# Seven products instead of eight in the second layer of the last half of expert 3, normalising at another place, and a new table of moves

## The chip, the cores and the metric

The kernel runs on one core of a Trainium2 chip. The metric is the device time of one execution in microseconds (us), median of three runs. The core's engines run side by side, each through its own queue in order: PE (TensorE, matrix products), DVE (VectorE), ACT (ScalarE), POOL (GpSimd) and SP (SyncE, which issues most DMAs). They wait for each other through semaphores only.

## What is computed

Linear attention, a mixture of four experts ("first MoE"), and a two-layer network with an ELU ("second MoE"), one after the other:

```python
q_s = softmax(q over head_dim);  k_s = softmax(k over seq)          # 4 x 8 heads, 576 x 64
x = q_s @ (k_s.T @ v)                                               # -> 2304 tokens x 512
p = domain_probs / (domain_probs.sum(-1, keepdims=True) + 1e-09)    # 2304 x 4
for e in range(4):
    out += p[:, e:e + 1] * (relu(x @ w1[e]) @ w2[e])                # 512 -> 1024 -> 512
h = out @ w_in                                                      # 512 -> 2048
g = where(h > 0, h, exp(min(h, 0)) - 1)
result = g @ w_out                                                  # 2048 -> 512
```

## The kernel before

All matrix operands stand as pairs of a high and a low part, so each product of 128x128 weights with a block of tokens takes three matmuls (high x high, high x low, low x high). Sums are kept transposed (features on partitions) in one big tile, `accs`.

**The opening** does the attention (`START` and the hooks of `at(n, ...)`) beside expert 0, which runs over 7 blocks of 256 tokens and one of 512 without any saving of products. `matmul` counts columns and calls `hook()` after each 2048 of them; `at(n, fn)` puts `fn` at the n-th hook (a hook is about 1 us of PE). `normalise` divides the expert probabilities by their sum, in four small DVE instructions (L757 to L760); it stands at hook 10. `p_turn` (hook 150) transposes what it made and stores it to DRAM (`prow`).

**The main loop** has 30 steps, `STEPS`: `s` from 0 to 9, each with three token blocks `b` of 768 (step number i = 3 s + b). An `s` is half a unit, that is 4 slices of 128 hidden features: s = 0 to 5 are experts 1 to 3, s = 6 to 9 the second MoE. `S_MOE` is 6 and `S_FAST` is 5. In each step PE does the first layer of its own block by seven products (Strassen, `PRODUCTS`, done for each of two halves `fp` = 0, 1: 2 x 7 x 6 = 84 matmuls of 384 columns, line L1458), and between these the second layer of the step before, cut in pieces (`fill`):

- plain (`group`, L1546 to L1548): 8 groups of 12 matmuls, 96 in all. Before, s = 5 and the first block of s = 6 are done so.
- by seven products (`second_product`, L1670, or `turned_product`, L1583, in the second MoE): 7 x 12 = 84 matmuls. It needs sums and differences of quarters of the hidden values and of the second weights: `quarter_a11`, `direct`, `quarter_a21`, `quarter_a12`, `late_parts` for the values, and `w2_fast` for the weights. What comes out is weighted with `pb` and added to `accs` by DVE, or by DVE and POOL ("part").

The list `SEVEN` says which `s` are done by seven. Plain ones take their second weights whole, split in `w2_step`.

**Between the MoEs** the sums in `accs` become the next input. `own_steps(b)` does this for each block in seven pieces (B11, B21, T3, B22, T2, T4, T1): `hi` (L1226) makes the high part on ACT, `lo` (L1234) the low part on DVE or POOL, `diff` (L1242 to L1256) the differences in place on POOL, `keep` (L1262) stores each part to DRAM for the later steps. Block b's pieces stand in the second half of the step ahead of (s = 6, b) and in the first half of that step. A place in the ring of eight pieces is written again only when its store has read it.

The order on every engine is that in which the program is written out; the scheduler is off. Positions are counted in hooks (`at`), in `SH` = 24 places per step (`at2`, `hook2`) and in products (`drain`). The table `MOVES` shifts single operations by some places, or gives them another engine ('d' DVE, 'p' POOL, 'a' ACT).

A bank of PSUM that PE has filled is read by ACT and DVE before PE may write it again; so every sum, ReLU or ELU that is late holds PE a few products later. In the second MoE the ELU of one quarter is three ACT instructions (`elu`, L1500 to L1502) and two or more on DVE (`rest`, L1511 to L1518).

Of the kernel before, what the change touches and what calls it, by code (L numbers as in the profile page):

```python
# [62 lines left out]
    ('spe', 2, 14): 'd', ('spe', 2, 2): 'd', ('sprd', 0, 3): -0.5, ('sprd', 1, 10): 1, ('sprd', 1, 11): 1,  # L63
    ('sprd', 1, 12): 1, ('sprd', 1, 13): 1, ('sprd', 1, 14): 1, ('sprd', 1, 15): 1, ('sprd', 1, 16): 1,
    ('sprd', 1, 17): 1, ('sprd', 1, 4): 1, ('sprd', 1, 5): 1, ('sprd', 1, 6): 1, ('sprd', 1, 7): 1, ('sprd', 1, 8): 1,
    ('sprd', 1, 9): 1, ('sprd', 2, 10): 0.5, ('sprd', 2, 11): 0.5, ('sprd', 2, 12): 0.5, ('sprd', 2, 13): 0.5,
    ('sprd', 2, 14): 0.5, ('sprd', 2, 15): 0.5, ('sprd', 2, 16): 0.5, ('sprd', 2, 17): 0.5, ('sprd', 2, 5): 0.5,
    ('sprd', 2, 6): 0.5, ('sprd', 2, 7): 0.5, ('sprd', 2, 8): 0.5, ('sprd', 2, 9): 0.5, ('sumlo', 'T2'): 'p',
# [37 lines left out]
def tile_attention_moe_moe(  # L106
# [963 lines left out]
    def w2_step(s, p):  # L1070
# [6 lines left out]
        if s == S_MOE:  # L1077
            now = hook2_n[0] - NB * S_FAST * SH
            for n in range(2):
                at2(NB * S_FAST, now + 3 + n, lambda n=n: sums_of(r, p, n), "sm", p, n)  # L1080
# [808 lines left out]
```

## Time and profile before

| | |
|---|---|
| median of three runs | 1176.66 us (1175.61 to 1178.84) |
| the profiled execution, its own time | 1175.68 us |
| its span in the trace | 1173.7 us |
| busy share | PE 98%, DVE 81%, POOL 56%, ACT 54% |
| opening, until the first product of the loop | 261 us |
| one step of 84 + 84 matmuls without loss | 29.12 us |

A busy share of 98% is not 98% of work: matmuls overlap, and the end of each is modelled. What tells more is how many matmuls start in a stretch: at full pace those of 384 columns start every 173 ns. Steps that take longer than that have lost time.

### The profile page before, as it was taken

What the parts mean: (1) busy time and instruction counts of PE and PEld (TensorE: products, weight loads), DVE (VectorE), ACT (ScalarE), POOL (GpSimd) and SP (SyncE); (2) the same over time, 40 slices, a digit from 0 to 9 for tenths busy, and PEclk for the clock granted to TensorE, in tenths of its full rate; (3) what the DMA queues carried; (4) which work ended last, traced back from release to release, by engine and by line L of the source; (5) the groups of instructions that cost most, each with busy time, mean ns of one, the idle gap of its engine ahead of it and who ended that gap; (6) DMA issues with size and microseconds to landing.
All of it is one profiled execution on the core that took longest, in us unless ns stands there. A gap on an engine that the chain in (4) does not pass through costs nothing. (4 is left out here: it accounts for less than half of the span.)

```text
span 1173.7 us, 20319 instructions
## 1 busy us (share of the span) xinstructions
PE 1148.1 (98%) x7234; PEld 1127.7 (96%) x7234; DVE 949.9 (81%) x1514; ACT 638.5 (54%) x1348; POOL 659.1 (56%) x559
## 2 busy tenths in 40 slices
PE   8899999999999999999999999999989999999998
PEld 7899999989999999999999999999979999999998
DVE  8977888676887887898998987686478879879876
ACT  7544543325455455455455443245688767767763
POOL 5521543447578578577578572155755646646643
PEclk9999999999999999999999999999999999999999
DMA  9356565867677777767867869643575465565462
GB/s 287 121 151 197 164 216 189 297 232 267 243 252 268 273 244 277 275 233 281 293 238 269 301 222 326 240 186 115 187 247 194 180 251 206 196 235 207 180 242 108
DMA packets 124728, 266.76 MB, mean 227 GB/s; under 512 B 12428, under 2 KB 48980, under 8 KB 124628
## 3 DMA queue, kind: packets, MB, share of 16 engines
q1 hardware_dynamic: 122900, 262.33, 63.8%
q10 hardware_dynamic: 1728, 3.15, 0.7%
q8 instruction: 57, 0.93, 0.3%
q14 instruction: 43, 0.35, 0.1%
HBM read 218.21 MB, written 47.22 MB: 226 GB/s over the span
## 5 line engine op out<-in xcount | busy, mean ns | idle before, releaser
L1458 PE MATMUL m<-xh,w1s 128*128 128x384 f32 x840 | 246.5, 338 | 9.1 <-DVE half L1512 4.0
L1458 PE MATMUL h<-xh,w1s 128*128 128x384 f32 x840 | 243.7, 335 | 3.5 <-DVE half L1517 1.2
L1458 PEld LDWEIGHTS m<-xh,w1s 128*128 128x128 f32 x840 | 155.1, 189 | 13.4 <-DVE half L1512 4.3
L1458 PEld LDWEIGHTS h<-xh,w1s 128*128 128x128 f32 x840 | 154.3, 188 | 5.2 <-ACT m L1747 1.8
L1458 PE MATMUL m<-xl,w1s 128*128 128x384 f32 x420 | 141.3, 336 | 0.0
L1458 PE MATMUL h<-xl,w1s 128*128 128x384 f32 x420 | 140.6, 335 | 0.0
L1288 PE MATMUL o<-hpa,w2t 128*128 128x256 f32 (+1 forms) x768 | 119.8, 300 | 0.8 <-DVE hpa L1321 0.7
L1288 PE MATMUL h<-xh,w1t 128*128 128x256 f32 (+1 forms) x512 | 112.0, 298 | 0.0
L1288 PEld LDWEIGHTS o<-hpa,w2t 128*128 128x128 f32 x768 | 104.3, 191 | 5.5 <-DVE hpa L1321 1.0
L1696 POOL TENSOR_TENSOR accs<-part,accs 128x768 f32<-128x768 f32 x35 | 69.2, 1977 | 63.0 <-DVE part L1695 60.3
L1288 PEld LDWEIGHTS h<-xh,w1t 128*128 128x128 f32 x512 | 86.2, 192 | 2.5
L995 POOL TENSOR_TENSOR w2g<-r,w2g 128x512 fp32r<-128x512 f32 x54 | 73.8, 1378 | 14.9 <-ACT w2g L994 14.0
L1670 PE MATMUL o<-xh,w2g 128*128 128x384 f32 x360 | 79.8, 334 | 0.0
L1458 PEld LDWEIGHTS m<-xl,w1s 128*128 128x128 f32 x420 | 79.4, 189 | 0.2
L1458 PEld LDWEIGHTS h<-xl,w1s 128*128 128x128 f32 x420 | 78.8, 188 | 0.1
L1670 PE MATMUL o<-hpa,w2g 128*128 128x384 f32 x360 | 78.5, 335 | 0.0
L1670 PE MATMUL o<-xl,w2g 128*128 128x384 f32 x360 | 77.9, 335 | 0.0
L1288 PE MATMUL h<-xl,w1t 128*128 128x256 f32 (+1 forms) x256 | 77.5, 303 | 0.1
L1596 DVE TENSOR_TENSOR accs<-o,accs 128x768 f32<-128x768 f32 (+1 forms) x69 | 62.6, 908 | 4.7 <-PE o L1583 4.6
L1670 PEld LDWEIGHTS o<-hpa,w2g 128*128 128x128 f32 x360 | 63.8, 188 | 0.4 <-DVE o L1689 0.4
L1670 PEld LDWEIGHTS o<-xh,w2g 128*128 128x128 f32 x360 | 64.0, 188 | 0.0
L1670 PEld LDWEIGHTS o<-xl,w2g 128*128 128x128 f32 x360 | 63.7, 188 | 0.1
(364 smaller groups left out, 3002.8 us busy)
## 6 DMA issues: line engine op xcount, KB each, us to landing
xh<-xs SPq DMA_DIRECT2D x189, 384.0 KB, 6.4
xl<-xs SPq DMA_DIRECT2D x189, 384.0 KB, 6.8
xs<-xh SPq DMA_DIRECT2D x42, 384.0 KB, 3.5
xs<-xl SPq DMA_DIRECT2D x42, 384.0 KB, 3.8
r<-in_w_dram SPq DMA_DIRECT2D x56, 256.0 KB, 4.2
extra<-prow SPq DMA_DIRECT2D x38, 192.0 KB, 6.0
r<-scratch SPq DMA_DIRECT2D x24, 256.0 KB, 4.8
x<-in_w_in_dram SPq DMA_DIRECT2D x11, 512.0 KB, 6.0
```

The lines of the kernel that those rows point to most:

```text
L995: eng_of(nc.gpsimd, "w2lo", cls(s), op).tensor_tensor(out=t[:, 1], in0=src, in1=t[:, 0].bitcast(F32), op=ALU.subtract)
L1288: nc.tensor.matmul(out, lhsT, rhs, **kw)
L1458: nc.tensor.matmul(dst, t[:, wl, c + dl, :], x[xl_][:, dl, :], start=(n == 0 and p < 2), stop=(n == 5), skip_group_check=True,)
L1596: nc.vector.tensor_tensor(out=a, in0=x, in1=a, op=ALU.add)
L1670: nc.tensor.matmul(o[:, m], l, r, start=(k < 2 and n == 0), stop=(n == 5), skip_group_check=True)
L1696: nc.gpsimd.tensor_tensor(out=a, in0=r, in1=a, op=ALU.add)
```

## The change

Four edits:

- `SEVEN[s]` is now true for all s but 6. The second layer of s = 5 (steps 15 to 17) is done by `second_product`, its values by the quarters of the first MoE, its weights by `w2_fast`. The scratch tiles of step 17's last products are taken from `gt`, since the ELU of step 18 already uses the usual ones.
- The plain weights of s = 6 were loaded and split ahead of their step, during s = 5; now they are loaded and split in step 18 itself (`w_load(s, ., 1)`, `w2_step`, and behind it `sums_of`).
- `normalise` goes from hook 10 to hook 120. The last three conversions of second-MoE weights from 64-bit words use their usual tiles instead of `gt`.
- `MOVES` is laid out anew: 365 entries become 856, most with fractions of a place.

```diff
-    ('a11', 1, 1): 'd', ('ahead', 'E', 2, 0): 1, ('ahead', 'E', 2, 3): 1, ('ahead', 'E', 2, 8): 1,
+    ('a11', 1, 1): 'p', ('a11', 2, 1): 'd', ('ahead', 'M', 0, 1): 1, ('ahead', 'M', 0, 2): 1, ('ahead', 'M', 0, 6): 1,
...
-    SEVEN = [s < S_FAST or s > S_MOE for s in range((NU - 1) * FPU // FS)]
+    SEVEN = [s != S_MOE for s in range((NU - 1) * FPU // FS)]
...
-    at(10, normalise)
+    at(120, normalise, "nrm")
...
         if s == S_MOE:
-            now = hook2_n[0] - NB * S_FAST * SH
+            now = hook2_n[0] - NB * S_MOE * SH
             for n in range(2):
-                at2(NB * S_FAST, now + 3 + n, lambda n=n: sums_of(r, p, n), "sm", p, n)
+                at2(NB * S_MOE, now + 3 + n, lambda n=n: sums_of(r, p, n), "sm", p, n)
...
-    CONV += [(later, end1 + t, 1, True) for t in (11, 22, 33)]
+    CONV += [(later, end1 + t, 1, False) for t in (11, 22, 33)]
...
-            a2, b2, c2, d2, a1, b1 = (2, 13, 25, 29, 34, 38)
-            if s > 0 and (s <= S_FAST or SEVEN[s]):
+            a1, b1 = (34, 38)
+            if s > 0:
                 at2(i, 2, lambda s=s: w_load(s, 0, 1), "l", k_, 0)
                 at2(i, 13, lambda s=s: w_load(s, 1, 1), "l", k_, 1)
                 if SEVEN[s]:
...
                     at2(i, 14, lambda s=s: w2_step(s, 0), "ws", k_, 0)
                     at2(i, 19, lambda s=s: w2_step(s, 1), "ws", k_, 1)
-                    a2, b2, c2, d2, a1, b1 = (23, 26, 30, 34, 41, 54)
...
-            if more and not SEVEN[s] and not SEVEN[s + 1]:
-                at2(i, a2, lambda s=s: w_load(s + 1, 0, 1), "l", k_, 2)
-                at2(i, b2, lambda s=s: w_load(s + 1, 1, 1), "l", k_, 3)
-                at2(i, c2, lambda s=s: w2_step(s + 1, 0), "ws", k_, 2)
-                at2(i, d2, lambda s=s: w2_step(s + 1, 1), "ws", k_, 3)
...
-        if s == S_FAST:
-            summed.add((b, th, m))
...
-            sums["s5"] = tmp.tile([P, 2, TB], F32, tag="qh", name="m5")
+            sums["s5"] = gt[:, :2] if i == NB * S_MOE - 1 else tmp.tile([P, 2, TB], F32, tag="qh", name="m5")
...
-                r = tmp.tile([P, 2, TB], F32, tag="ql", name="part")
+                r = gt[:, 2:] if i == NB * S_MOE - 1 else tmp.tile([P, 2, TB], F32, tag="ql", name="part")
```

The changed file has some 120 lines more ahead of the code, so its line numbers are higher: L1234 (`lo` of `own_steps`) becomes L1352, L1242 to L1256 (`diff`) L1360 to L1374, L1511 and L1512 (`rest`) L1629 and L1630, L1751 and L1762 (the two sums of the first layer) L1869 and L1880.

**Place 1: DVE in the opening, at hook 10.** Before, with `normalise` in L757 to L760; `xl<-m,xh` and `hpa<-m,hpa` split what PE has turned or multiplied for the attention.

```order
L1321 SCALAR_TENSOR_TENSOR hpa<-h,hpa 128x256
L336 TENSOR_REDUCE nm<-accs 128x1
L484 TENSOR_TENSOR hpa<-m,hpa 128x288
L757 TENSOR_REDUCE gx_93<-gx_93 128x18
L758 TENSOR_SCALAR gx_93<-gx_93 128x18
L759 RECIPROCAL gx_93<-gx_93 128x18
L760 TENSOR_TENSOR gx_93<-gx_93 128x18x4
L506 TENSOR_TENSOR xl<-m,xh 128x288
L1321 SCALAR_TENSOR_TENSOR hpa<-h,hpa 128x256
L506 TENSOR_TENSOR xl<-m,xh 128x288
L438 TENSOR_REDUCE qm<-accs 96x12
```

The changed kernel at the same place, and behind it the new place of `normalise` at hook 120 (L881 to L884).

```order
L460 TENSOR_REDUCE nm<-accs 128x1
L608 TENSOR_TENSOR hpa<-m,hpa 128x288
L577 TENSOR_REDUCE accs<-accs 96x6
L578 TENSOR_SCALAR accs<-accs 96x6
L579 RECIPROCAL accs<-accs 96x6
L1439 SCALAR_TENSOR_TENSOR hpa<-h,hpa 128x256
L671 TENSOR_TENSOR w1t<-r,w1t 128x512
L608 TENSOR_TENSOR hpa<-m,hpa 128x288
L630 TENSOR_TENSOR xl<-m,xh 128x288
L562 TENSOR_REDUCE qm<-accs 96x12
L1439 SCALAR_TENSOR_TENSOR hpa<-h,hpa 128x256
L630 TENSOR_TENSOR xl<-m,xh 128x288
```

```order
L1439 SCALAR_TENSOR_TENSOR hpa<-h,hpa 128x256
L550 SCALAR_TENSOR_TENSOR kvs<-m,ks,kvs 64x64 x2
L1439 SCALAR_TENSOR_TENSOR hpa<-h,hpa 128x256
L881 TENSOR_REDUCE gx_93<-gx_93 128x18
L882 TENSOR_SCALAR gx_93<-gx_93 128x18
L883 RECIPROCAL gx_93<-gx_93 128x18
L884 TENSOR_TENSOR gx_93<-gx_93 128x18x4
L562 TENSOR_REDUCE qm<-accs 96x12
L483 TENSOR_TENSOR ek<-m,ek 128x640
L957 TENSOR_TENSOR xl<-sum,xh 128x2x384
```

The four instructions have left the place ahead of the splits (L506, now L630), a weight split (L671) stands nearer there, and they now stand among q's and k's late steps.

**Place 2: POOL from the second half of step 18 on.** Before: `own_steps` of block 1 (L1234, L1242 to L1256) between the splits of the ELU (L1482, `parts`).

```order
L1234 TENSOR_TENSOR xl<-accs,xh 128x768
L1482 TENSOR_TENSOR xh<-half,xh 128x384
L1242 TENSOR_TENSOR accs<-accs 128x768
L1234 TENSOR_TENSOR xl<-accs,xh 128x768
L1247 TENSOR_TENSOR accs<-accs 128x768
L1252 TENSOR_TENSOR accs<-accs 128x768
L1234 TENSOR_TENSOR xl<-accs,xh 128x768
L1482 TENSOR_TENSOR xl<-half,xl 128x384
L1234 TENSOR_TENSOR xl<-accs,xh 128x768
L1482 TENSOR_TENSOR xh<-half,xh 128x384
L1482 TENSOR_TENSOR hpa<-half,hpa 128x384
L1256 TENSOR_TENSOR accs<-accs 128x768
```

The changed kernel, the same stretch (L1199 `w2_step`, L1143 `sums_of`, L1814 the weighted part of step 17's second layer, L1600 `parts`, L1352 and L1370 `own_steps`).

```order
L1600 TENSOR_TENSOR hpa<-half,hpa 128x384
L1199 TENSOR_TENSOR w2s<-r,w2s 128x512 x2
L1143 TENSOR_TENSOR r<-r 128x256 x2
L1814 TENSOR_TENSOR accs<-gt,accs 128x768
L1370 TENSOR_TENSOR accs<-accs 128x768
L1600 TENSOR_TENSOR xl<-half,xl 128x384
L1600 TENSOR_TENSOR xh<-half,xh 128x384
L1352 TENSOR_TENSOR xl<-accs,xh 128x768
L1600 TENSOR_TENSOR xh<-half,xh 128x384
L1352 TENSOR_TENSOR xl<-accs,xh 128x768
L1600 TENSOR_TENSOR gx<-half,gx 128x384
L1352 TENSOR_TENSOR xl<-accs,xh 128x768
```

Of the eleven instructions of block 1 four are left on POOL (three `lo`, one `diff`); over the three blocks 19 become 9. The split of the weights of s = 6 and part of the new second layer have come in.

**Place 3: DVE in the second half of step 18.** Before (L1554 and L1555 weight and add the plain second layer of step 17).

```order
L1511 SCALAR_TENSOR_TENSOR m<-m,half 128x384
L1512 SCALAR_TENSOR_TENSOR half<-half,m 128x384
L1554 TENSOR_TENSOR o<-o,extra 128x384
L1555 TENSOR_TENSOR accs<-o,accs 128x384
L1554 TENSOR_TENSOR o<-o,extra 128x384
L1555 TENSOR_TENSOR accs<-o,accs 128x384
L1751 TENSOR_TENSOR m<-h,extra 128x384
L1762 TENSOR_TENSOR h<-h,extra 128x384
L1511 SCALAR_TENSOR_TENSOR m<-m,half 128x384
L1512 SCALAR_TENSOR_TENSOR half<-spare,m 128x384
L1554 TENSOR_TENSOR o<-o,extra 128x384
```

The changed kernel (L1809, L1810, L1807 and L1813 are the second layer by seven; L1143 is `sums_of`).

```order
L1143 TENSOR_TENSOR r<-r 128x256 x4
L1629 SCALAR_TENSOR_TENSOR m<-m,half 128x384
L1630 SCALAR_TENSOR_TENSOR half<-half,m 128x384
L1352 TENSOR_TENSOR xl<-accs,xh 128x768
L1360 TENSOR_TENSOR accs<-accs 128x768
L1809 TENSOR_TENSOR o<-o,extra 128x2x384
L1810 TENSOR_TENSOR accs<-o,accs 128x768
L1869 TENSOR_TENSOR m<-h,extra 128x384
L1807 TENSOR_TENSOR o<-o,gt 128x2x384
L1813 TENSOR_TENSOR gt<-o,extra 128x768
L1352 TENSOR_TENSOR xl<-accs,xh 128x768
L1880 TENSOR_TENSOR h<-h,extra 128x384
```

The ELU's pairs (L1511 and L1512, now L1629 and L1630) stand behind more and longer instructions than before, among them `own_steps`.

## Rows read from the trace of the kernel before

**Rows 1.** The page: span and instructions.

```profile
span 1173.7 us, 20319 instructions
```

**Rows 2.** Stretches: length; busy PE, PEld, DVE, ACT, POOL (instructions); clock, DMA share, GB/s.

```profile
485.36:514.48 29.12, 29.12 (x170) 29.12 (x170) 26.65 (x40) 14.94 (x30) 18.27 (x14) 1.00 0.75 263
543.60:691.84 148.24, 147.16 (x842) 145.30 (x842) 132.12 (x187) 73.57 (x152) 100.80 (x78) 1.00 0.79 282
691.84:786.20 94.36, 92.80 (x529) 91.31 (x529) 69.37 (x116) 33.65 (x67) 32.81 (x26) 1.00 0.68 241
786.20:818.17 31.97, 31.51 (x181) 31.19 (x181) 23.27 (x42) 17.99 (x37) 17.76 (x15) 1.00 0.40 155
818.17:855.99 37.82, 33.27 (x181) 32.63 (x181) 17.28 (x28) 26.36 (x56) 29.51 (x22) 0.95 0.53 186
855.99:892.54 36.55, 31.55 (x169) 30.59 (x169) 30.61 (x48) 29.59 (x64) 21.41 (x21) 0.95 0.74 262
```

**Rows 3.** Timeline of PE, ACT, DVE and POOL in the opening: start, us, what.

```profile
37.60 0.40 PE L1288 MATMUL h<-xh,w1t 128*128 128x256 f32 x2
41.89 0.74 PE L469 MATMUL m<-ident,accs 96*128 96x96 f32 x3 [3.90 <-DVE xl L506]
...
37.41 0.40 ACT L502 ACTIVATE xh<-m 128x288 fp32r<-128x288 f32 x1
...
36.30 4.60 DVE L758 TENSOR_SCALAR gx<-gx 128x18 f32<-128x18 f32 x1
...
41.38 0.45 DVE L506 TENSOR_TENSOR xl<-m,xh 128x288 fp32r<-128x288 f32 x1
...
35.73 1.30 POOL L547 TENSOR_TENSOR w1t<-r,w1t 128x512 fp32r<-128x512 f32 x1
...
39.60 1.26 POOL L547 TENSOR_TENSOR w2t<-gt,w2t 128x512 fp32r<-128x512 f32 x1
```

**Rows 4.** Stretches of PE alone: length, busy us (matmuls), granted clock, DMA share, GB/s.

```profile
41.62:45.02 3.40, 3.13 (x15) 0.50 0.00 0
823.30:826.60 3.30, 3.27 (x10) 0.50 0.82 320
860.90:864.20 3.30, 3.30 (x12) 0.50 0.62 240
```

**Rows 5.** POOL alone near hook 120: length, busy us (instructions), clock, DMA.

```profile
174.10:178.10 4.00, 0.00 (x0) 1.00 0.27 98
```

**Rows 6.** Groups of DVE, shapes apart: line, what, count | busy us, mean ns | idle before.

```profile
L454 DVE TENSOR_SCALAR qs<-qs 96x12 f32<-96x12 f32 x12 | 2.0, 169 | 0.4
L1691 DVE TENSOR_TENSOR o<-o,extra 128x768 f32<-128x768 f32 x25 | 24.0, 959 | 10.4 <-PE o L1670 10.4
L1511 DVE SCALAR_TENSOR_TENSOR m<-m,half 128x384 f32<-128x384 f32 x48 | 26.8, 557 | 5.6 <-ACT spare L1501 3.4 <-ACT extra L1501 1.3 <-ACT half L1501 0.9
L1518 DVE TENSOR_TENSOR gt<-gt 128x384 f32<-128x384 f32 x22 | 18.9, 859 | 0.0
L1234 DVE TENSOR_TENSOR xl<-accs,xh 128x768 fp32r<-128x768 f32 x14 | 17.3, 1245 | 9.6 <-ACT xh L1226 9.4
L948 DVE TENSOR_TENSOR w1s<-r,w1s 128x512 fp32r<-128x512 f32 x35 | 29.5, 844 | 2.4 <-ACT w1s L933 2.4
L948 DVE TENSOR_TENSOR w1s<-r,w1s 128x256 fp32r<-128x256 f32 x18 | 12.5, 695 | 0.0
```

**Rows 7.** The same view of POOL, for the split that DVE has as L1234.

```profile
L1234 POOL TENSOR_TENSOR xl<-accs,xh 128x768 fp32r<-128x768 f32 x7 | 12.8, 1836 | 1.0 <-ACT xh L1226 1.0
```

**Rows 8.** Waits: who waited for whom: us in total, times, longest us.

```profile
ACT xh L1226 <- POOL accs L1242: 8.6, 3, 4.2
PE m L1458 <- DVE half L1512: 4.0, 1, 4.0
PE m L1458 <- DVE half L1517: 3.2, 1, 3.2
```

**Rows 9.** DMA issues: what, count, KB each, us to landing.

```profile
xs<-xh SPq DMA_DIRECT2D x42, 384.0 KB, 3.5
```

More of the change, by code (lines that the diff above doesn't have):

```diff
@@ L21 @@
 MOVES = {
[41 rows of a table removed]
[L63 to L68, printed above, removed]
[33 rows of a table removed]
[90 rows of a table added]
+    ('spe', 2, 13): 'p', ('spe', 2, 14): 'd', ('spe', 2, 2): 'p', ('spe', 2, 8): 'd', ('sprd', 0, 1): -0.485,
+    ('sprd', 0, 10): 0.024, ('sprd', 0, 11): 0.105, ('sprd', 0, 17): -0.113, ('sprd', 0, 2): 0.253,
+    ('sprd', 0, 3): -0.5, ('sprd', 0, 5): -0.529, ('sprd', 0, 8): 0.167, ('sprd', 1, 0): 1.288, ('sprd', 1, 1): 5.272,
+    ('sprd', 1, 10): 2.072, ('sprd', 1, 11): 5.479, ('sprd', 1, 12): 3.534, ('sprd', 1, 13): 3.286,
+    ('sprd', 1, 14): 2.288, ('sprd', 1, 15): 2.331, ('sprd', 1, 16): 2.288, ('sprd', 1, 17): 1.32,
+    ('sprd', 1, 2): 3.644, ('sprd', 1, 3): 3.297, ('sprd', 1, 4): 3.285, ('sprd', 1, 5): 1.538, ('sprd', 1, 6): 1.139,
+    ('sprd', 1, 7): 2.132, ('sprd', 1, 8): 3.846, ('sprd', 1, 9): 2.801, ('sprd', 2, 0): 0.312, ('sprd', 2, 1): 0.804,
+    ('sprd', 2, 10): 1.516, ('sprd', 2, 11): 1.516, ('sprd', 2, 12): 2.503, ('sprd', 2, 13): 1.516,
+    ('sprd', 2, 14): 1.548, ('sprd', 2, 15): 1.516, ('sprd', 2, 16): 1.371, ('sprd', 2, 17): 1.516,
+    ('sprd', 2, 2): 1.278, ('sprd', 2, 3): 1.079, ('sprd', 2, 4): 0.977, ('sprd', 2, 5): 1.412, ('sprd', 2, 6): 0.55,
+    ('sprd', 2, 7): 1.516, ('sprd', 2, 8): 1.516, ('sprd', 2, 9): 0.697, ('sumlo', 'T1'): 'p', ('sumlo', 'T2'): 'p',
[103 rows of a table added]
 }
@@ L998, in w2_sum @@
     def w2_sum(s, op):
-        b11, b12, b21, b22 = (w2_raw(s, o) for o in ("B11", "B12", "B21", "B22"))
-        o, x, y = {
-            "T1": (b11, b12, b11), "T3": (b12, b12, b22), "T2": (b22, b22, b11), "T4": (b21, b21, b22),
-        }[op]
+        o, x, y = (w2_raw(s, n) for n in {
+            "T1": ("B11", "B12", "B11"), "T3": ("B12", "B12", "B22"), "T2": ("B22", "B22", "B11"),
+            "T4": ("B21", "B21", "B22"),
+        }[op])
         st_ = w2st.setdefault(s, {o: o for o in ("B11", "B12", "B21", "B22")})
@@ L1684, in second_product @@
             th, mh = GOES[k]
+            if s == S_FAST:
+                summed.update((b, th, 2 * mh + m) for m in range(2))
             a, p = acc_turned(b, th, mh), over(pb[:, th], 2)
```

263 rows, old and new, of the table MOVES are left out of this document.

## Prediction

> **What bounds the kernel now.** I first looked at PE over the whole span [rows 1], stretch by stretch [rows 2]. PEld there is the loading of weights. A step in the middle, with 84 + 84 = 168 matmuls of 384 columns, takes 29.12 us, so one starts every 173.3 ns, and a step with a plain second layer (84 + 96 = 180) would take 31.20 us (the counts in the rows are one or two higher, from matmuls that reach into the stretch). Against that pace the stretches of the loop lose: steps 10 to 14 (148.24 us against 5 x 29.12) 2.6 us; steps 15 to 17 (94.36 against 528 x 0.1733 = 91.5) 2.8 us; step 18 0.8 us; step 19 (37.82 against 31.20) 6.6 us, and step 20 (36.55 against 29.12) 7.4 us. So PE bounds the loop by its columns alone, but for the change from the first to the second MoE, steps 18 to 20, which loses 14.8 us.
>
> Then I asked what ended the longest waits of PE. In the opening PE has nothing running from 38.0 to 41.9 us [rows 3]: it waits 3.90 us for DVE's split L506, which stands behind L758, an addition of a constant to 18 columns that took 4.60 us. POOL worked through that whole time (35.73 to 40.86 us: four times L547 and a small memset between), and L758 ended at 40.90, right behind POOL's last. The same form with nothing on POOL takes 0.17 us (L454) [rows 6]. In steps 19 and 20 PE waits 4.0 and 3.2 us for ELU instructions of DVE [rows 8]; these were late since ACT stood behind `hi`, waiting for POOL's `diff` (8.6 us in three waits), and POOL had a queue of splits and differences of 1.84 us each [rows 7]. Behind each of the three long gaps the granted clock is 0.5, the lower level of 1.2 GHz, for some 3.4 us [rows 4], with 10 to 12 matmuls where 19 fit at 173 ns: about 1.6 us more each time.
>
> **The change part by part.**
>
> *Fewer products.* The second layers of steps 15 to 17 lose 12 matmuls each: 36 x 0.1733 = 6.2 us of PE. PE is the bound there, so this counts in full: -6.2.
>
> *`normalise`.* Its four instructions leave the spot where they held PE. Gone are the wait of 3.9 us and the slow clock behind it (3.40 us at half speed from 41.62 on, 1.6 us lost): 5.5 us. Next late is L506 itself: ACT's high part is there at 37.8 us (L502) [rows 3], so DVE would be through at 38.3, when PE has just finished; 0.3 us stay. At hook 120, near 175 us, DVE's four instructions cost 0.2 + 0.2 + 0.3 + 0.3 = 1 us if POOL is quiet. Before, it idled there for 4 us [rows 5]; in the new order POOL's last instruction ahead of them (L585) is written some 5,000 columns of PE earlier, its next (L951) some 4,000 later, about 2 us each way. `p_turn` waits for them only at hook 150. I take -5.2; the bounds are -5.5 and, if L758 (now L882) met a busy POOL again and PE stood behind it, +0 (the 5.5 us only moved).
>
> *Steps 15 to 17 by seven.* They become what steps 10 to 14 are, in PE's work and in that of the other engines, but step 15 still has its three conversions beside the new preparation. Steps 10 to 14 lose 0.5 us each, the three now lose 2.8 together, so about 1 us less; steps 10 to 14 themselves keep their order but for shifts by fractions: I take -0.8 for both, bounds -4 (nothing lost any more) and +2 (one long wait like that of rows 8, in step 15, at two thirds).
>
> *The transition.* Here the change cuts both ways, and it is the largest unknown. POOL loses ten of its 19 pieces of `own_steps`: 10 x 1.84 = 18.4 us, which was the queue that ACT waited for. DVE gets them at 1.25 us each (L1234) [rows 6], and more: by the order of the changed kernel, step 18 holds on DVE 9 instructions of 768 columns out of PSUM (9 x 0.96 = 8.6), 8 pieces of `own_steps` (8 x 1.25 = 10.0), 19 of 384 columns with an operand in PSUM, the ELU's among them (19 x 0.557 = 10.6), 4 of 384 out of SBUF (4 x 0.86 = 3.4), 3 weight splits of 512 columns (3 x 0.84 = 2.5) and 5 weight pieces of 256 (5 x 0.70 = 3.5): 38.6 us in a step of 29.1, where 23.3 us were busy before [rows 2]. A part of it is the split of the weights of s = 6 and `sums_of`, which were done in steps 15 to 17 and are now queued ahead of the ELU. Step 19 holds 31 us by the same prices in 31.2. So DVE alone is 9 us over PE's time; PE runs on for two or three us when a sum or an ELU is late, which leaves 6 to 7 us of waiting in steps 18 and 19. Spread over many waits it need not lower the clock; I add 0.8, half a lowering. In step 20 DVE's and POOL's queues are short again, but the ELU, `hi` and the splits of ACT fill 30 us as before; of its 7.4 us I keep 4. Together 11.5 in place of 14.8: -3.3. Bounds: -12 (loss 3, rival 1) and +16 and more (rival 2).
>
> One shift by itself: the store of block 0's T3 goes back by 14 products, to the start of step 19, and ACT's `hi` for block 1 writes that place a product later, after the store has read it. A store takes 3.5 us from its issue [rows 9], and ACT's ELU stands behind it; it falls into DVE's lag, so I count it there at nothing. With DVE on time it would cost up to 3.
>
> *Sum.* -6.2 - 5.2 - 0.8 - 3.3 = -15.5, against the profiled execution's 1175.68 us (span 1173.7 and 2 around it): 1160.2. The median of the runs is 1.0 us above that execution, so 1161.2 as a median.
>
> **A rule against it.** DVE's instructions with an operand in PSUM keep their 0.557 and 0.96 us, while those with both in SBUF vary: 0.86 for the 384 columns that cost 0.557 from PSUM, 1.25 for 768 [rows 6]. The Trainium skill ("SBUF — State Buffer", section "Who interferes with whom") says that a DVE instruction with two SBUF inputs contends with a GpSimd instruction that reads SBUF, that tensor_scalar can do so too, and that the later one blocks until the first has finished; "Perfetto Trace Analysis" (section "Optimizing Scalar/DVE Operations") concludes that moving work between those two might not help. By that rule the transition gains nothing from its new engines; the trace agrees as to L758, which was blocked for 4.60 us [rows 3], longer than any single POOL instruction.
>
> **The rivals.**
>
> 1. *The transition clears.* If the queue that matters was POOL's alone, and DVE's work of step 18 is taken up where it has air (by the same prices 24 us in step 17, 25 in step 20), the losses fall to those of ordinary steps, 3 us in all instead of 14.8: -11.8. Then 1176.66 - 6.2 - 5.2 - 0.8 - 11.8 = 1152.7. For it: L1234 on DVE is a third shorter than on POOL, and the chain of high part, low part and difference is a third shorter with it. Against it: 38.6 us of DVE in 29.1.
>
> 2. *DVE waits for POOL at each piece, and the kernel gets slower.* Steps 18 and 19 have 32 instructions on DVE with both operands in SBUF, 17 of them of 768 columns. If each of the 17 takes POOL's 1.84 instead of 1.25 and the 15 others grow by the same half, DVE needs 17 x 0.59 + 15 x 0.4 = 16 us more, 86 in 60. PE then waits 23 us there after what it can run on, the clock falls twice (3.2), and step 20 keeps its 7.4: 34 against 14.8, so +19. With -6.2 and -5.2 this is 1184. It decides the sign once the transition loses over 27 us. For it: POOL is still busy 26 us in step 18 by count, so there is always something to collide with. Against it: the mean of 1.25 already holds such collisions.
>
> 3. *The transition only keeps its loss,* DVE in POOL's place, with the same two long gaps and slow clocks: 14.8 to 20 us or somewhat more. Then 1176.66 - 6.2 - 5.2 + 0 to +5 = 1165 to 1170.
>
> 4. *`normalise` takes its wait along*: the 5.5 us come back near 175 us. With all else as forecast 1166.7.
>
> **How the numbers follow.** Forecast (transition loses 7 to 15 us): 0.50, at 1161, alone 1156 to 1166. Rival 1: 0.22. Rival 3: 0.17. Rival 4: 0.05. Rival 2 and anything like it: 0.06. A measurement here tells about 0.3%, 3.5 us, from no change, so same is 1173.1 to 1180.2: that takes losses in the transition of 23 to 30 us, 0.05, from the upper end of rival 3 (0.03) and the lower of rival 2 (0.02); slower 0.04, the rest of rival 2; faster 0.91. The range of 8 in 10 reaches from somewhat below rival 1's time to a little above the upper end of rival 3: 1150 to 1171.
>
> **What will show it.** L1546 to L1548 as `group` (now L1664 and its neighbours) with 96 matmuls instead of 384, and steps 15 to 17 at about 29.5 us. No wait over 1 us on PE near 40 us, clock 1.0 there, and L882 below 0.3 us. In steps 18 and 19 DVE over 85% busy, POOL less than before, PE's waits now on DVE with ACT and POOL done long before; the mean of L1352 on DVE near 1.25. Wrong it would be if DVE is not full in step 18 (rival 1), if L1352 on DVE nears 1.84 (rival 2), or if the gain in the opening comes back as waits for another splitting of q or k, since the order of all of these was shifted too.

## The result and the profile after

The changed kernel takes 1166.13 us (median of four runs, 1164.73 to 1168.53) against 1177.38 us of the kernel before in the same comparison: a ratio of 0.9907, 95% interval 0.9885 to 0.9929, so 11 us less. The forecast was 1161 (range 1150 to 1171); direction and range held, and the gain came out about a quarter smaller than forecast. The span fell from 1173.7 [rows 1] to 1164.2 us.

The same view of stretches as [rows 2], of the changed kernel (columns: length; busy PE, PEld, DVE, ACT, POOL with instructions; clock; DMA share; GB/s): steps 10 to 14, steps 15 to 17, then 18, 19 and 20 by themselves.

```profile
544.64:692.27 147.63, 147.42 (x842) 145.42 (x841) 132.13 (x192) 72.92 (x151) 96.12 (x75) 1.00 0.82 280
692.27:781.07 88.80, 88.23 (x505) 87.11 (x505) 76.56 (x109) 46.48 (x95) 57.94 (x46) 1.00 0.64 217
781.07:818.41 37.34, 32.45 (x169) 30.57 (x169) 33.97 (x50) 24.45 (x50) 26.09 (x20) 0.95 0.42 154
818.41:853.29 34.88, 31.77 (x181) 31.13 (x181) 27.91 (x43) 28.89 (x61) 22.41 (x17) 1.00 0.76 278
853.29:883.22 29.93, 29.56 (x169) 29.06 (x169) 23.66 (x38) 26.39 (x58) 26.32 (x26) 1.00 0.75 271
```

With 173.3 ns per matmul (168 of them make 29.12 us, 180 make 31.20) this gives what each stretch loses, beside the terms of the prediction. The loop began at 261.06 us before and at 261.57 after (start of its first matmul), and the trace counts 7198 matmuls in place of 7234.

| term | forecast | measured in the two traces |
|---|---|---|
| 36 matmuls fewer | -6.2 | -6.2 |
| opening (`normalise`) | -5.2 | +0.5 |
| losses of steps 10 to 17 | -0.8 | -2.0 (5.5 to 3.5) |
| losses of steps 18 to 20 | -3.3 | -2.1 (14.8 to 12.7: 8.2, 3.7, 0.8) |
| the other steps | 0 | +0.3 |
| sum | -15.5 | -9.5 (span) |

Nearly all of the miss is in one line: the opening gave nothing (5.7 of the 6.0 us by which the two sums differ). There the timeline (start us, us, what, idle before and releaser) has this in place of [rows 3]:

```profile
35.68 0.83 POOL L585 TENSOR_TENSOR accs<-accs 96x384 f32<-96x384 f32 x1 [0.39 <-DVE accs L579]
35.76 5.12 DVE L671 TENSOR_TENSOR w1t<-r,w1t 128x512 fp32r<-128x512 f32 x1
36.47 1.27 POOL L671 TENSOR_TENSOR w2t<-r,w2t 128x512 fp32r<-128x512 f32 x1
37.68 0.20 POOL L472 MEMSET accs<- 128x128 f32 x1
37.85 1.26 POOL L671 TENSOR_TENSOR w1t<-gt,w1t 128x512 fp32r<-128x512 f32 x1
39.07 1.26 POOL L671 TENSOR_TENSOR w2t<-gt,w2t 128x512 fp32r<-128x512 f32 x1
40.80 0.45 DVE L608 TENSOR_TENSOR hpa<-m,hpa 128x288 fp32r<-128x288 f32 x1
41.30 1.09 PE L617 MATMUL m<-hpa,kvs 128*128 128x288 f32 x3 [4.40 <-DVE hpa L608]
```

`normalise` is gone, and a weight split (L671, w1t of slice 5), which the new table gives to DVE, takes its place: 5.12 us instead of 0.68 (the mean of L671 for `w2t<-r` on DVE), until POOL's row of splits is over. This is no wait for a semaphore: the trace shows DVE as busy in L671 all that time, so here an engine held another up by other means than the semaphores. PE waits 4.40 us for the split behind it. The stretch 39.60 to 46.40 of the changed kernel shows the clock behind that: 0.50 throughout (1.2 of 2.4 GHz), for 6.8 us, where before it was 3.4 us [rows 4].

```profile
39.60:46.40 6.80, 5.10 (x24) 5.10 (x25) 4.77 (x8) 0.85 (x3) 2.41 (x3) 0.50 0.00 0
```

`normalise` itself did at its new place what was foretold; POOL's next instruction there begins at 178.10 us:

```profile
174.50 0.22 DVE L881 TENSOR_REDUCE gx<-gx 128x18 f32<-128x72 f32 x1
174.75 0.18 DVE L882 TENSOR_SCALAR gx<-gx 128x18 f32<-128x18 f32 x1
174.97 0.27 DVE L883 RECIPROCAL gx<-gx 128x18 f32<-128x18 f32 x1
175.26 0.28 DVE L884 TENSOR_TENSOR gx<-gx 128x72 f32<-128x72 f32 x1
```

In steps 18 and 19 the waits of PE (who waited for whom: us in total, times, longest), which answer to [rows 8]:

```profile
PE m L1576 <- DVE half L1630: 2.9, 1, 2.9
PE o L1786 <- POOL hpa L1729: 2.1, 1, 2.1
PE h L1576 <- DVE half L1630: 1.5, 1, 1.5
PE h L1576 <- ACT m L1865: 0.9, 1, 0.9
```

### The profile page after: what moved, and what is told of

It reads as the page before. It is cut to its first block, busy times and chain, and to the rows that moved or that the text cites. A ratio compares the mean times of both kernels' runs of the same rounds, so it can differ in the third digit from the quotient of the medians.

```text
span 1164.2 us, 20278 instructions
## 1 busy us (share of the span) xinstructions
PE 1142.3 (98%) x7198; PEld 1120.0 (96%) x7198; DVE 963.8 (83%) x1535; ACT 656.2 (56%) x1386; POOL 669.2 (57%) x570
## 5 line engine op out<-in xcount | busy, mean ns | idle before, releaser
L1814 POOL TENSOR_TENSOR accs<-part,accs 128x768 f32<-128x768 f32 x35 | 67.7, 1933 | 69.1 <-DVE part L1813 55.9
L1786 PE MATMUL o<-hpa,w2g 128*128 128x384 f32 x432 | 94.7, 336 | 2.1 <-POOL hpa L1729 2.1
L1786 PE MATMUL o<-xh,w2g 128*128 128x384 f32 x432 | 95.7, 336 | 0.0
L1786 PE MATMUL o<-xl,w2g 128*128 128x384 f32 x432 | 93.3, 334 | 0.0
L1119 POOL TENSOR_TENSOR w2g<-r,w2g 128x512 fp32r<-128x512 f32 x56 | 80.9, 1453 | 12.0 <-ACT w2g L1118 12.0
L1786 PEld LDWEIGHTS o<-hpa,w2g 128*128 128x128 f32 x432 | 77.1, 189 | 2.4 <-POOL hpa L1729 2.4
L1786 PEld LDWEIGHTS o<-xh,w2g 128*128 128x128 f32 x432 | 77.1, 189 | 0.1
L1786 PEld LDWEIGHTS o<-xl,w2g 128*128 128x128 f32 x432 | 76.5, 188 | 0.2 <-DVE o L1798 0.2
```

The source lines that it names most:

```text
L1119: eng_of(nc.gpsimd, "w2lo", cls(s), op).tensor_tensor(out=t[:, 1], in0=src, in1=t[:, 0].bitcast(F32), op=ALU.subtract)
L1786: nc.tensor.matmul(o[:, m], l, r, start=(k < 2 and n == 0), stop=(n == 5), skip_group_check=True)
L1814: nc.gpsimd.tensor_tensor(out=a, in0=r, in1=a, op=ALU.add)
```

## The experiments

All ratios are against the kernel before, run on the same chip; times are medians. The runs were made in several series on different chips; the kernel before took 1177.4, 1176.5, 1176.0 and 1175.9 us in them, so times of different series can be compared to about 1 us.

### What held PE in the opening

Theory A: a row of POOL instructions without a gap blocks the next DVE instruction of an exposed kind until the row ends, whichever it is; `normalise` was only the one that stood there. Theory B: PE would have waited at that place anyway. First, `normalise` alone, in the kernel before:

```diff
-    at(10, normalise)
+    at(120, normalise)
```

> The kernel before, with normalise at hook 120 instead of 10 and nothing else changed. In the changed kernel the wait near 40 us is still there (4.4 us in place of 3.9), now behind a weight split (L671) on DVE that took 5.12 us while POOL worked through its row of splits; before, normalise's addition stood there. Theory A: POOL's row of splits blocks whichever DVE instruction with all its operands in SBUF comes next, and the old table has none other there (behind normalise come the splits L506, which read PSUM). Then the wait and the slow clock behind it go: about 1172.2 us, 5.2 less than before, no wait of PE over 1 us near 40 us, clock 1.0 there. Theory B: something else holds PE there anyway (the high part on ACT, the next weights), and normalise alone is worth nothing: 1176 to 1178 us, with a wait of 3 to 5 us near 40 us.

Measured: 1171.43 us, ratio 0.9966 (0.9951 to 0.9981): 5.1 us less, as theory A and the prediction's own term have it. PE, without a gap in 36 to 41 us (before: 2.00 of 5.00), beside a POOL busy for all of it:

```profile
36.00:41.00 5.00, 5.00 (x45) 5.00 (x44) 3.70 (x9) 3.37 (x10) 5.00 (x6) 1.00 0.35 111
```

So the edit was worth what the prediction said, in the order of the kernel before. Then the other side, one entry of the new table turned back:

```diff
-    ('wlo', 5, 0): 'd',
+    ('wlo', 5, 0): 'p',
```

> The changed kernel with one entry of its table turned: the low part of the first-layer weights of slice 5 (w1t, L671 near 36 us) on POOL, where it was before, instead of DVE. Theory A (as for the kernel before with normalise moved): the wait of 4.4 us and the slow clock behind it go, less up to 1.3 us for one split more in POOL's row: 1160 to 1162 us, 4.5 to 5.5 less than the changed kernel; DVE has no instruction over 2 us between 35 and 42 us. Theory B: 1165 to 1167 us, another wait at the same place. A third way: POOL's row, now five splits long, makes the weights of slice 6 late, and PE waits for L671 on POOL: 1163 to 1166 us.

Measured: 1158.89 us, ratio 0.9860 (0.9839 to 0.9881). That is 7.2 us less than the changed kernel, more than the 4.5 to 5.5 expected, since the slow clock of 6.8 us went too: the loop begins at 254.89 instead of 261.57 us, 6.7 us sooner, of which 4.4 are the gap in PE and some 2 the clock. This version beats both kernels. The stretch 36 to 41 us in the changed kernel (first) and here (second):

```profile
36.00:41.00 5.00, 0.90 (x8) 0.70 (x6) 5.00 (x2) 1.40 (x3) 4.33 (x5) 0.86 0.32 107
```

```profile
36.00:41.00 5.00, 5.00 (x44) 5.00 (x43) 4.52 (x9) 3.59 (x9) 5.00 (x6) 1.00 0.42 120
```

POOL is busy for all of the second row too, and DVE does nine instructions in it. So it is not POOL's work as such that stops DVE; it matters what stands on DVE meanwhile. Here these are (groups of that stretch: count, busy us, mean ns):

```profile
L562 DVE TENSOR_REDUCE qm<-accs 96x12 f32<-96x768 f32 x2 | 1.9, 938 | 0.0
L630 DVE TENSOR_TENSOR xl<-m,xh 128x288 fp32r<-128x288 f32 x2 | 0.9, 451 | 0.0
L608 DVE TENSOR_TENSOR hpa<-m,hpa 128x288 fp32r<-128x288 f32 x2 | 0.9, 450 | 0.1
```

The two-operand ones have one operand in PSUM (`m`), and TENSOR_REDUCE has a single input: none was held up. The two that were, L758 and L671, are a TENSOR_SCALAR and a TENSOR_TENSOR with all operands in SBUF.

Next `normalise` back at hook 10, without and with the split on DVE:

```diff
-    at(120, normalise, "nrm")
+    at(10, normalise)
```

> The changed kernel with the split of slice 5 on POOL (1158.9 us so far) and normalise back at hook 10. Theory A (a row of POOL instructions without a gap blocks the next DVE instruction of the exposed kinds until the row ends; PE then loses the wait and the slow clock behind it): POOL's row is five splits here, L882 comes behind its start and takes about 5 us, PE waits 4 to 5 us, clock 0.5 behind it: 1164 to 1167 us, as the changed kernel. If instead normalise is harmless in the new order: 1159 to 1160 us.

> The changed kernel with normalise back at hook 10 and nothing else. Theory A: it stands behind the split that is blocked already, runs when POOL's row is over and costs only its own 0.8 to 1 us there: 1166 to 1168 us, so that the move of normalise by itself is worth next to nothing in the changed kernel, though it was worth 5.1 us in the kernel before. If the two costs add up: 1171 to 1173 us.

Measured: 1165.95 us (ratio 0.9920, 0.9899 to 0.9942) with the split on POOL, 1166.88 us (0.9929, 0.9909 to 0.9950) with it on DVE. In the first the victim is `normalise` again, for the length of POOL's row, which is four splits and a memset (the expectations count one split too many):

```profile
36.23 5.23 DVE L882 TENSOR_SCALAR gx<-gx 128x18 f32<-128x18 f32 x1
```

in the second it runs in 0.18 us behind the split that has sat the row out. With the runs above this makes a table of two by two:

| | split of slice 5 on DVE | on POOL |
|---|---|---|
| `normalise` at hook 10 | 1166.9 | 1166.0 |
| `normalise` at hook 120 | 1166.1 (the change) | 1158.9 |

Either edit alone is worth nothing that can be told; only both together clear the place. The last of these runs makes POOL's row one split shorter:

```diff
-    ('wlo', 6, 0): 'p',
+    ('wlo', 6, 0): 'd',
```

> The changed kernel with one of the splits in POOL's row (w1t of slice 6) given to DVE: the row is one instruction of 1.26 us shorter. Theory A: the blocked split of slice 5 on DVE takes 5.12 - 1.26 = 3.9 us (to the end of the row), PE waits about 3.1 us instead of 4.4, and with the slow clock lasting as long or half as long the time is 1162.5 to 1165 us. If an instruction is blocked only by the one POOL instruction that it meets (a fixed cost, or something else that holds DVE there): 5.1 us as before, 1166 to 1167 us.

The blocked split shrinks as theory A has it, by the one split that left POOL's row, and PE's wait with it:

```profile
36.45 3.90 DVE L671 TENSOR_TENSOR w1t<-r,w1t 128x512 fp32r<-128x512 f32 x1
37.16 1.27 POOL L671 TENSOR_TENSOR w2t<-r,w2t 128x512 fp32r<-128x512 f32 x1
...
38.53 1.26 POOL L671 TENSOR_TENSOR w2t<-gt,w2t 128x512 fp32r<-128x512 f32 x1
...
40.77 1.09 PE L617 MATMUL m<-hpa,kvs 128*128 128x288 f32 x3 [3.17 <-DVE hpa L608]
```

The time, 1166.03 us (0.9912, 0.9889 to 0.9935), missed the 1162.5 to 1165 expected. In the profiled execution the loop begins at 261.39 us, 0.2 sooner than in the changed kernel: PE's first transposes came 0.5 us later, and the slow clock lasted 6.8 us again, of which PE now worked through 6.24, not 5.10:

```profile
40.20:47.00 6.80, 6.24 (x29) 6.24 (x30) 5.95 (x10) 1.98 (x5) 1.85 (x3) 0.50 0.01 2
```

The mechanism shows in the trace; a gain in time does not.

So theory A holds at this place. It is not a rule for every row of POOL, and the same traces show it. In the changed kernel 49 DVE TENSOR_TENSORs with both operands in SBUF met a POOL instruction that had another TENSOR_TENSOR within 0.1 us behind it, and took at least 0.25 us longer than the shortest of their shape. Only two of them sat out more than one of these POOL instructions: L671 here, and one near 180 us. The other 47 were through before POOL's next had ended, and that one took on average 0.4 us longer than the shortest of its shape. This is the usual picture, in step 2 of the loop:

```profile
323.88 1.85 POOL L1814 TENSOR_TENSOR accs<-part,accs 128x768 f32<-128x768 f32 x1 [2.20 <-DVE part L1813]
...
324.76 1.39 DVE L1760 TENSOR_TENSOR gt<-gt 128x384 f32<-128x384 f32 x1
325.68 1.34 POOL L1729 TENSOR_TENSOR xh<-gt,xh 128x384 fp32r<-128x384 f32 x1
326.07 1.50 DVE L1072 TENSOR_TENSOR w1s<-r,w1s 128x512 fp32r<-128x512 f32 x1
...
326.99 1.47 POOL L1729 TENSOR_TENSOR hpa<-gt,hpa 128x384 fp32r<-128x384 f32 x1
```

DVE and POOL take turns here, though POOL has no gap. What decides between the two pictures no run here shows.

### Code or table

The new code with the old table, and the old code with the new table (`normalise` at hook 120 in both), to stand beside the kernel before with `normalise` at 120 and the changed kernel. The first diff is against the changed kernel, the second against the kernel before:

```diff
 MOVES = {
-    ('a11', 1, 1): 'p', ('a11', 2, 1): 'd', ('ahead', 'M', 0, 1): 1, ('ahead', 'M', 0, 2): 1, ('ahead', 'M', 0, 6): 1,
+    ('a11', 1, 1): 'd', ('ahead', 'E', 2, 0): 1, ('ahead', 'E', 2, 3): 1, ('ahead', 'E', 2, 8): 1,
...
```

> The changed kernel's code with the table of the kernel before: seven products in steps 15 to 17, the weights of s = 6 split in step 18, normalise at hook 120, but own_steps on POOL as before and no shift of the new table. By the terms of the prediction: products -6.2, normalise -5.2 (the old table puts no weight split of DVE at that place), steps 10 to 17 about 0, so 1166 us if the transition keeps its 14.8 us. Theory C (own_steps on DVE was needed, POOL's queue gets the split of the weights on top): the transition loses 20 to 30 us, 1171 to 1181 us. Theory D (the table does little at the transition): 12 to 16 us, 1163 to 1167 us.

```diff
 MOVES = {
-    ('a11', 1, 1): 'd', ('ahead', 'E', 2, 0): 1, ('ahead', 'E', 2, 3): 1, ('ahead', 'E', 2, 8): 1,
+    ('a11', 1, 1): 'p', ('a11', 2, 1): 'd', ('ahead', 'M', 0, 1): 1, ('ahead', 'M', 0, 2): 1, ('ahead', 'M', 0, 6): 1,
...
-    at(10, normalise)
+    at(120, normalise, "nrm")
```

> The kernel before with the new table and normalise at hook 120: all of the change but the second layer of steps 15 to 17 (eight products there, and the weights of s = 6 split during s = 5 instead of in step 18). If the 36 products count in full, 6.2 us more than the changed kernel in steps 15 to 17. Theory C (the split of the weights and the sums in step 18 overload DVE there): step 18 loses 3 us or less instead of 8.2, so the whole is 1166 to 1169 us. Theory D (the losses of steps 18 and 19 come from own_steps and the ELU alone): step 18 loses as much as in the changed kernel, 1171 to 1174 us. The wait near 41 us stays, with the weight split.

| | old table | new table |
|---|---|---|
| eight products in steps 15 to 17 | 1171.4 | 1174.4 |
| seven | 1195.1 | 1166.1 (the change) |

(Ratios 1.0164, 1.0141 to 1.0186, for the seven with the old table; 0.9988, 0.9976 to 0.9999, for the eight with the new one. The right column holds the blocked split of the opening, 5 to 7 us.) With the old table the edit that saves 36 matmuls costs 24 us. Steps 15 to 19 of that run, one by one:

```profile
686.92:720.12 33.20, 30.63 (x170) 28.82 (x169) 25.71 (x36) 15.75 (x32) 24.04 (x20) 1.00 0.62 205
720.12:752.18 32.06, 30.05 (x170) 28.96 (x169) 29.86 (x42) 15.11 (x31) 19.54 (x15) 1.00 0.82 287
752.18:787.27 35.09, 31.55 (x169) 30.59 (x169) 27.02 (x30) 16.21 (x33) 28.16 (x20) 0.95 0.38 146
787.27:835.00 47.73, 36.57 (x169) 34.23 (x169) 32.08 (x43) 23.39 (x47) 31.35 (x23) 0.86 0.35 128
835.00:876.50 41.50, 34.22 (x181) 33.58 (x181) 21.62 (x31) 26.55 (x56) 30.13 (x23) 0.92 0.51 184
```

Steps 15 to 17 lose 13 us and step 18 loses 18.6: both theories C and D were too low. The new code puts the split of the weights of s = 6, the sums and the second layer by seven into step 18; in the old order ACT, DVE and POOL wait for each other there (ACT 6.3 us for DVE and 6.2 for POOL, DVE 6.2 for ACT, POOL 6.8 for ACT, in single waits). With the old code and the new table the transition is quieter than in the changed kernel (step 18 loses 4.1 us, step 19 2.5), nearer to theory C (3 or less) than to theory D (8.2). The time is not theory C's 1166 to 1169 us, though: step 16 loses 8.2 us, 4.1 in one wait of PE for ACT, which had itself waited 8.3 us for a DMA; no theory had that. The two edits are one: the table pays for what the products move.

### The pieces of `own_steps`

All twenty entries that choose the engine of a low part or a difference are taken out of the table:

```diff
-    ('xde', 0, 1): 'd', ('xde', 0, 3): 'd', ('xde', 0, 4): 'p', ('xde', 1, 1): 'd', ('xde', 1, 2): 'p',
...
-    ('xle', 0, 'B21'): 'd', ('xle', 0, 'B22'): 'p', ('xle', 0, 'T2'): 'd', ('xle', 0, 'T4'): 'd',
...
```

> The changed kernel with every low part and difference of own_steps on the engine of the kernel before (19 on POOL instead of 9, DVE's L1365 and two of L1352 less): this prices the ten pieces that went to DVE. By the prediction's transition (POOL's queue of 1.84 us a piece was what ACT and PE waited for) the ten pieces put 18 us on POOL, and steps 18 to 20 lose 18 to 30 us instead of 12.7: 1171 to 1183 us. Theory E (DVE is the bound of steps 18 and 19, and is relieved of 10 to 12 us): 10 us or less are lost, 1158 to 1164 us.

Measured: 1179.31 us, ratio 1.0032 (1.0021 to 1.0042), 13 us more than the changed kernel; steps 17 to 20 lose 27.2 us instead of 13.3. Theory E, with 1158 to 1164 us, is out. ACT again waits for POOL's differences, as in [rows 8], and longer:

```profile
ACT xh L1344 <- POOL accs L1360: 12.8, 3, 6.1
ACT xh L1344 <- POOL accs L1370: 3.9, 1, 3.9
```

So moving the ten pieces from POOL to DVE was worth 13 us, although DVE is the fuller of the two in step 18 (33.97 us busy of 37.34, against 26.09).

### Can the transition be made shorter by single shifts?

Three shifts on top of the split on POOL: the low part for which PE waits 2.1 us near 787 (`s1`), the weight split of s = 6 later (`w2`), one difference behind the ELU for which PE waits 2.9 us (`d3`); in this order in the diff.

```diff
-        late_parts((s1, g22, "S1", bcls(i), fp))
+        if i == NB * S_MOE - 1 and fp:
+            nc.scalar.activation(out=s1[0], in_=g22, func=AF.Copy)
+        else:
+            late_parts((s1, g22, "S1", bcls(i), fp))
         relu_with(t3, h, g11, ALU.subtract)
         nc.vector.tensor_tensor(out=t2, in0=g22, in1=g11, op=ALU.subtract)
+        if i == NB * S_MOE - 1 and fp:
+            nc.vector.tensor_tensor(out=s1[1], in0=g22, in1=s1[0].bitcast(F32), op=ALU.subtract)
...
-    ('sm', 0, 0): 3.067, ('ws', 6, 0): -5.95,
+    ('sm', 0, 0): 0.717, ('ws', 6, 0): -3.6,
...
-    ('xd', 1, 3): 1.993,
+    ('xd', 1, 3): 3.3,
```

> The changed kernel with the split of slice 5 on POOL (1158.9 us), and in step 17's hidden values one low part (the S1 of the second half, L1729) on DVE behind the two sums there, instead of on POOL. In the changed kernel PE waits 2.1 us near 787 us for this L1729, which stood on POOL behind L1072, L1078 and L1079 (781.6 to 785.4 us) though its high part was there at 782.9. Theory F (the order of POOL's queue makes this wait): on DVE it is there near 784.5, the wait goes, DVE is 0.55 us later: step 18 loses 4 to 5 us instead of 6.4 to 8.2, 1156 to 1158 us. Theory G (step 18 is bound by DVE's sum, so a wait removed comes back at the next sum): 1158 to 1160 us.

> The kernel of the run above, and the split of the weights of s = 6 in step 18 put 2.35 places later (its loads stay), so that ACT doesn't stand 1.2 and 1.0 us waiting for their landing ahead of an ELU. Theory F: the ELU near 802 us is 1 to 1.5 us earlier and PE's wait of 1.5 us near 804 is halved or gone: another 0.8 to 1.5 us less, 1155 to 1157 us. Theory G: DVE's queue holds PE as long as before, no difference within 1 us.

> The kernel with L1729 on DVE, and one difference of own_steps (block 1's third, L1365, 0.98 us on DVE) put behind the ELU for which PE waits 2.9 us near 822 us. Theory G (DVE's queue in front of that ELU is the wait): the wait is 1 us shorter, 0.9 to 1.1 us less than without it, or 2 if the clock stays up. If the ELU was held by ACT: no difference, or 1 us more, since the high part that needs the difference comes later.

> All three shifts together, with the split of slice 5 on POOL. If each removes its own wait they add up: 1153 to 1156 us. If DVE's sum over steps 18 and 19 is the bound (theory G), they do not, and it stays within 1.5 us of the best single one: 1156 to 1158 us.

Measured: 1159.35 (s1), 1160.35 (s1 and w2), 1159.11 (s1 and d3), 1158.56 us (all), ratios 0.9862, 0.9869, 0.9864 and 0.9858, each with an interval of about 0.003 either way; without any of them 1158.89 (0.9860). None can be told from none. Theory F's times were missed each time, theory G's only with all three shifts (1156 to 1158 us, by 0.6), and the gain of 0.9 to 1.1 us expected of d3 cannot be seen in the time. The waits of PE in steps 18 to 20 with s1 show why:

```profile
PE m L1576 <- DVE half L1630: 2.9, 1, 2.9
PE h L1576 <- DVE half L1630: 1.5, 1, 1.5
PE o L1791 <- DVE accs L1815: 0.9, 1, 0.9
PE m L1576 <- DVE h L1874: 0.6, 1, 0.6
```

The wait for POOL is gone, and two new ones for DVE stand in its place (L1815 and L1874 are L1810 and L1869 of the changed kernel); step 18 loses 7.0 us as against 6.4. With w2 step 18 loses 1.0 us less, but the 2.9 us of the next step became 3.7 and the slow clock behind them lasted 6.8 us instead of 3.4. With d3 the 2.9 us became 2.0, as expected, in step 18 nothing changed, and 0.8 us less in step 19 is below what the times resolve. DVE in step 18 of s1 (which runs from 774.86 to 810.95):

```profile
774.00:810.00 36.00, 31.60 (x167) 28.22 (x166) 34.35 (x51) 24.20 (x49) 22.90 (x20) 1.00 0.42 158
```

34.35 us of 36.00: this fits theory G, a sum of work on DVE that is longer than PE's 29.12 us. Some 2.7 us of it are not work but DVE held up beside POOL (an estimate: five instructions, by what they took above the shortest of their shape), and what is left is still longer. Over the nine versions that keep this order but for single shifts (the changed kernel, four of the opening, four here), steps 18 and 19 together lose 10.6 to 12.8 us: the waits moved and did not go. Less of DVE's work in step 18 was run only with other things changed: with eight products in steps 15 to 17 that step has 27.85 us of DVE and loses 4.1 us, at the price in step 16; with the pieces of `own_steps` on POOL it has 30.81 and loses 7.6, at the price of POOL's longer queue. So that DVE alone is the bound there is likely, not shown.

## Why the prediction came out as it did

- **Fewer products: right.** Twelve matmuls fewer stand in each of steps 16, 17 and 18, where these second layers are done. Steps 15 to 17 take 88.80 us in place of 94.36: 24 matmuls less are 4.2 us of it, the other 1.4 are losses that went; PE stayed the bound there. In step 18 the 2.1 us of the last twelve are drowned in its waits.
- **`normalise`: the step that failed.** The mechanism was read rightly (POOL's row held L758, PE stood behind it), its price also (5.1 us measured in the order of the kernel before), and the new place costs nothing, as said. What failed is the sentence "Next late is L506 itself". It asked what came next in the old order, and there it was right: with `normalise` moved in the kernel before, PE has no gap. In the new order, which stood ahead of the prediction (place 1), a weight split with both operands in SBUF comes next on DVE, and a row of three splits on POOL still runs beside it. The prediction took the one victim for the cause. The bound of +0 was given, with a wrong reason: the wait did not travel with `normalise` (rival 4, at 0.05), it stayed and took another. The last sentence on what would make it wrong, the gain coming back as waits for other splits of q or k, came nearest.
- **Steps 10 to 17: right in sign, too small** (-2.0 for -0.8). The wait of 1.0 us in step 10 is gone and steps 16 and 17 run like 13 and 14; inside the bounds. (The lower bound, nothing lost any more, should have been -5.4 and not -4, by the prediction's own losses of 2.6 and 2.8 us.)
- **The transition: right in direction, 1.2 us off** (12.7 for 11.5), **partly by luck.** DVE is busy 91% of step 18 (over 85% was forecast), ACT's waits for POOL's differences are gone, and shifts only move PE's waits from one instruction of DVE to another. The split among the steps was other than thought: step 20 lost 0.8 us, not 4, steps 18 and 19 together 11.9 instead of 7 to 8; the two errors cancel. The largest wait of step 18, 2.1 us, was for POOL, and with the slow clock behind it (3.4 us at half speed, about 1.7 lost) it is nearly half of that step's 8.2 in this trace. DVE's 38.6 us for step 18 were too much: the kinds come out and the counts within one, but the single times of its 49 instructions add up to 36.8 us, and since each starts a little before the one ahead has ended, DVE is busy for 34.0. So DVE is 5 us over PE's 29.1, not 9, and the two or three us that PE was to run on for do not show. Here is the group that rivals 1 and 2 hung on, of DVE and of POOL (mean in ns behind the busy us):

```profile
L1352 DVE TENSOR_TENSOR xl<-accs,xh 128x768 fp32r<-128x768 f32 x16 | 18.8, 1183 | 0.3 <-ACT xh L1344 0.3
...
L1352 POOL TENSOR_TENSOR xl<-accs,xh 128x768 fp32r<-128x768 f32 x5 | 10.0, 1997 | 3.3 <-ACT xh L1344 3.3
```

- That is 1.18 us against the forecast 1.25, far from rival 2's 1.84. Rival 1 fell: its sign of being right, a DVE that is not full in step 18, did not come.
- **The rule against it.** The rule of the Trainium skill ("Perfetto Trace Analysis", section "Optimizing Scalar/DVE Operations"), that work moved between DVE and GpSimd might not gain, was given little weight for the transition; the runs agree with that: the ten pieces are worth 13 us on DVE. In the opening the other rule of the Trainium skill ("SBUF — State Buffer", section "Who interferes with whom") was the thing to apply to the new order as well: it names which DVE instructions can be held up by GpSimd (those with two inputs in SBUF, and tensor_scalar in some forms; tensor_reduce never), and L671, L882 and L562 behaved so: 5.12, 5.23 and 0.94 us beside a busy POOL.
- **The store of T3** made ACT wait 2.2 us at 827 us, inside the 3.5 that were named, and no wait of PE follows from it, as counted.

The forecast of 1161 us was 5 us too low (6 between the two traces) because one term of -5.2 came out as +0.5; the smaller errors (+1.2 and -1.2) cancelled, which is luck.

## What to carry to other kernels

When an instruction is found to be blocked, ask what blocks it, and look in the new order for the next instruction of the same kind at that place: moving the victim away only helps if nothing else that can be held stands there. Test such a pair two by two; either edit alone may show nothing. And an edit that takes work from the bounding engine can cost several times its gain (here 24 us for 6) until the work that it moves onto the others has been spread anew.

## What was not expected of the hardware

- At this place of the opening a DVE instruction that met a row of POOL instructions without a gap was not let in between them: it took 5.12 us over a row of three splits and a memset behind the POOL instruction that it met, 3.90 us with one split less, and 5.23 us (`normalise`) over four splits and a memset. PSUM-reading TENSOR_TENSORs of the same queue kept 0.45 us beside a POOL that was busy for all of the 5 us. In 47 of 49 such meetings of TENSOR_TENSORs in the changed kernel DVE was let in behind the first POOL instruction; the cause of the difference stays open.
- The slow clock lasted 6.8 us behind PE's gap of 4.4 us in the changed kernel, and 3.4 us behind the 3.9 us of the kernel before; the 6.8 us cost some 2 us on top of the gap. The length is not set by the gap: the old code with the new table has the same gap of 4.4 us, and there the slow clock lasted 3.4 us. Behind PE's gap of 2.1 us near 787 us the clock fell in the changed kernel (to 0.50 for 3.4 us), and in the version with the split on POOL, with the same gap of 2.1 us, it did not; there it fell behind the gap of 2.9 us near 814 us, where the changed kernel kept it. So part of the loss of single steps (8.2 and 3.7 us in the one, 6.4 and 4.8 in the other) is where the clock fell in that execution.
